# Weaving the attention of a chunk with the MLP of the chunk before it, in a four-layer transformer kernel on one core

## Chip, cores, metric

One core of one Trainium2 chip. The metric is device time in microseconds (us) of one execution, the median of several runs; profile times come from one profiled execution and are some 1.5 us shorter.

## The reference

Four layers on x of 2048 x 512, in bfloat16: attention A, MLP B, A, B, each with a LayerNorm ahead and a residual addition behind.

```python
def A(x):   # linear attention, 32 heads of 16
    q, k, v = split(x @ wqkv)
    phi(u) = concat(softmax(u @ w_phi), softmax(-u @ w_phi))       # per head, 32 features
    kv, z = phi(k)^T v, sum over s of phi(k)                       # needs ALL rows of x
    o = (phi(q) kv) / (phi(q) z + 1e-6)
    return o @ wo
def B(x):   # F = 1376
    return (relu(x @ W_gate) * (x @ W_up)) @ W_down
x = x + A(ln(x)); x = x + B(ln(x)); x = x + A(ln(x)); x = x + B(ln(x))
```

Two dependences matter. kv is a sum over all rows, so no query can be finished before all keys of the layer are. All else goes row by row, so the MLP of 512 rows (a chunk) can start when the attention of those rows is done.

## The kernel before

x lies in SBUF as 16 tiles of 128 rows, four to a chunk. The layers are traced one after the other. A list scheduler at build time turns the trace into one fixed order for each engine; what is traced earlier has precedence, and what is ready may overtake. At run time each engine works down its list.

```python
def ln_stats_chunk(st, c):            # one chunk: statistics of 4 tiles, then one inverse root for all 4
    ...
    rsqrt_dve(st, rstd[:], ve[:], TPC)            # 10 small VectorE operations
    ...
def layer_A(st):
    ...                                           # keys of 4 chunks; per chunk the sums are added to kvzacc in SBUF
    for c in range(NC):
        ...                                       # queries of chunk c+1 (prologue)
        for ti in range(TPC):
            kvq = st.ps_q.tile([P, 3, 512], F32, name="qps", tag="q")     # 3 PSUM banks, one buffer
            ...                                   # 9 matmuls, then on VectorE: rS, Tn, U, dd, o
            for b in range(NDB):
                nc.tensor.transpose(out=otps[:, b, :], in_=o[:, b * P:(b + 1) * P], identity=st.ident[:])
            nc.scalar.copy(out=oT[:], in_=otps[:])
            ...                                   # yps = oT.T @ wo, 4 matmuls
            nc.vector.tensor_tensor(out=st.X[:, t, :], in0=st.X[:, t, :], in1=yps[:], op=Alu.add)
def layer_B(st):
    for c in range(NC):
        ln_transpose_chunk(st, c, xnTB)           # LayerNorm, transposes by DMA
        for f in range(NFT):
            ...                                   # gps, ups (8 matmuls), rg = relu(gps), ru = ups, hT = rg * ru
        for ti in range(TPC):
            ...                                   # yps = hT.T @ wd (11 matmuls), X += yps
...
    run_layers(st, ("A", "B", "A", "B"))
```

The softmax here doesn't subtract the row's maximum and nothing guards it: scores larger than these inputs give would overflow.

## Time and profile before

| | us |
|---|---|
| median of three runs | 561.69 |
| range | 560.95 to 563.63 |
| profiled span | 560.4 |
| key sums of layer 1 ready | 98 |
| key sums of layer 2 ready | 350 |

The prediction below shows the activity map, the table by stage and the groups. In the map each digit is the busy share of an engine in a slice of 14 us, in tenths. PE is TensorE, DVE VectorE, ACT ScalarE, POOL GpSimd, SP the queue that issues DMAs; PEclk is the granted TensorE clock in tenths. What matters is that attention keeps VectorE busy and the MLP keeps TensorE busy.

### The profile page before, as it was taken

To read this page: it belongs to the slowest core of one execution; us is meant where nothing else is said; L and a number is where in the kernel's file an instruction comes from. 1 tells how busy PE (TensorE), PEld (TensorE's weight loads), DVE (VectorE), ACT (ScalarE), POOL (GpSimd) and SP (SyncE) were. 2 spreads that over 40 slices of the span, in tenths; PEclk is the share of its full clock that TensorE was granted. 3 is DMA by queue.
4 is the path that set the end of the run, shared out by engine and by line. 5 is a ranking of instruction groups with operands and counts; after the bars stand their busy time and mean duration, and the time that the engine had idled before them with its cause. 6 is when DMAs were issued, how large, how long until landed. Compare 5 with 4: busy or idle time off the path is not lost.

```text
span 560.4 us, 6418 instructions
## 1 busy us (share of the span) xinstructions
PE 439.0 (78%) x2304; PEld 211.2 (38%) x2304; DVE 349.6 (62%) x859; ACT 214.6 (38%) x401; POOL 67.7 (12%) x48
## 2 busy tenths in 40 slices
PE   0167789665756999999998799565766999999993
PEld 0033344332332444444443454333332444444441
DVE  4746986899887644463628976898888732222221
ACT  0044557131410625354444557131401625344440
POOL 4002674000000000000002774000000000000000
PEclk9999999689875999999999999687865999999998
DMA  8804200000001110230100200000001220200004
GB/s 292 311 0 85 47 20 2 0 0 1 1 11 28 37 39 1 48 66 1 37 2 6 34 1 0 1 0 2 0 10 29 38 39 0 39 0 2 0 1 150
DMA packets 40400, 19.34 MB, mean 35 GB/s; under 512 B 35008, under 2 KB 39120, under 8 KB 40368
## 3 DMA queue, kind: packets, MB, share of 16 engines
q1 hardware_dynamic: 38992, 12.59, 10.3%
q0 software_dynamic: 1376, 6.34, 3.1%
q8 instruction: 18, 0.29, 0.2%
q14 instruction: 14, 0.11, 0.1%
HBM read 8.44 MB, written 2.10 MB: 19 GB/s over the span
## 4 chain that ended last, share of the span: by engine, by line
PE 58%; DVE 18%; ACT 8%; DMA 8%; POOL 3%; issue 3%; SPq 1%; ACTq 0%; POOLq 0%; DVEq 0%
PE ups L187 14%; PE gps L183 13%; PE yps L199 9%; PE yaps L316 8%; DMA X<-in_A_x_dram 4%; POOL phiK L234 3%; ACT oT L313 3%; DVE sk L231 3%; PE pqps L268 3%; DMA xnTB<-xn 3%; PE otps L311 2%; PE kvq L243 2%; DVE o L307 2%; PE qps L283 2%; DVE X L318 2%
## 5 line engine op out<-in xcount | busy, mean ns | idle before, releaser
L193 DVE TENSOR_TENSOR hT<-rg,ru 128x512 bf16<-128x512 bf16 (+1 forms) x88 | 37.3, 424 | 95.3 <-ACT ru L192 95.3
L234 POOL TENSOR_TENSOR phiK<-ek,sk 128x1024 bf16<-128x1024 bf16 x32 | 61.3, 1928 | 276.1 <-ACT vext L222 256.0
L183 PE MATMUL gps<-xnTB,wg 128*128 128x512 bf16 (+1 forms) x352 | 92.1, 385 | 0.0
L187 PE MATMUL ups<-xnTB,wu 128*128 128x512 bf16 (+1 forms) x352 | 91.7, 383 | 0.4 <-DVE X L201 0.2
L190 ACT ACTIVATE rg<-gps 128x512 bf16<-128x512 f32 (+1 forms) x88 | 52.5, 597 | 85.8 <-PE gps L183 85.1
L199 PE MATMUL yps<-wd,hT 128*128 128x512 bf16 (+1 forms) x352 | 77.9, 379 | 1.8 <-DVE X L201 1.8
L316 PE MATMUL yaps<-wo,oT 128*128 128x512 bf16 x128 | 47.3, 509 | 24.2 <-ACT oT L313 24.2
L192 ACT CAST ru<-ups 128x512 bf16<-128x512 f32 (+1 forms) x88 | 51.5, 585 | 33.2 <-PE ups L187 33.2
L313 ACT COPY oT<-otps 128x512 bf16<-128x512 bf16 x32 | 19.1, 595 | 112.7 <-PE otps L311 112.7
L187 PEld LDWEIGHTS <-wu 128*128 128x128 bf16 (+1 forms) x352 | 35.2, 100 | 45.5 <-issue 4.4
L183 PEld LDWEIGHTS <-wg 128*128 128x128 bf16 (+1 forms) x352 | 35.8, 102 | 42.8 <-issue 3.2
L199 PEld LDWEIGHTS <-hT 128*128 128x128 bf16 (+1 forms) x352 | 34.4, 98 | 43.8 <-issue 2.6
L153 DVE BATCH_NORM_STATS2 bnst<-X 128x6 f32<-128x512 bf16 x64 | 43.3, 680 | 11.6 <-DMA X<-in_A_x_dram 11.2
L298 DVE TENSOR_TENSOR Tn<-qps,rS 128x1224 bf16<-128x1224 f32 x32 | 45.0, 1406 | 0.1
L168 DVE TENSOR_SCALAR xn<-X,mv,rstd 128x512 bf16<-128x512 bf16 x64 | 33.5, 535 | 17.4 <-DMA xnTB<-xn 11.8
L231 DVE TENSOR_REDUCE sk<-ek 128x64 f32<-128x1024 bf16 x32 | 38.2, 1195 | 6.5 <-ACT ek L229 6.2
L283 PE MATMUL qps<-R,EqT 128*128 128x144 bf16 x288 | 31.3, 270 | 13.6 <-DVE Tn L298 13.6
L220 PE MATMUL vps<-wqkv,xnTA 128*128 128x512 bf16 x128 | 36.2, 387 | 2.7 <-DMA xnTA<-xn 2.7
L201 DVE TENSOR_TENSOR X<-X,yps 128x512 bf16<-128x512 bf16 x32 | 21.8, 683 | 25.7 <-PE yps L199 25.7
L283 PEld LDWEIGHTS <-EqT 128*128 128x128 bf16 x288 | 26.4, 120 | 24.1 <-DVE Tn L298 16.5
L311 PE MATMUL otps<-ident,o 128*128 128x128 bf16 x128 | 15.2, 254 | 24.6 <-DVE o L307 24.6
L318 DVE TENSOR_TENSOR X<-X,yaps 128x512 bf16<-128x512 bf16 x32 | 22.0, 688 | 20.0 <-PE yaps L316 19.9
(60 smaller groups left out, 438.8 us busy)
## 6 DMA issues: line engine op xcount, KB each, us to landing
X<-in_A_x_dram SPq DMA_DIRECT2D x4, 512.0 KB, 9.6
out_dram<-X SPq DMA_DIRECT2D x1, 2048.0 KB, 7.5
wqkv<-in_A_wqkv_dram POOLq DMA_DIRECT2D x1, 1536.0 KB, 10.6
wg<-in_B_W_gate_dram POOLq DMA_DIRECT2D x1, 1376.0 KB, 14.3
wu<-in_B_W_up_dram POOLq DMA_DIRECT2D x1, 1376.0 KB, 17.7
wd<-in_B_W_down_dram POOLq DMA_DIRECT2D x1, 1280.0 KB, 20.8
wo<-in_A_wo_dram POOLq DMA_DIRECT2D x1, 512.0 KB, 11.5
xnTA<-xn SPq DMA_TRANSPOSE x32, 2.4
```

The costliest lines, as they stand in the source:

```text
L153: nc.vector.bn_stats(out=stats[:], in_=st.X[:, t, :])
L183: nc.tensor.matmul(gps[:fsz, :], lhsT=st.wg[:, b, f * P:f * P + fsz], rhs=xnTB[:, b, :], start=(b == 0), stop=(b == NDB - 1))
L187: nc.tensor.matmul(ups[:fsz, :], lhsT=st.wu[:, b, f * P:f * P + fsz], rhs=xnTB[:, b, :], start=(b == 0), stop=(b == NDB - 1))
L190: nc.scalar.activation(out=rg[:fsz, :], in_=gps[:fsz, :], func=AF.Relu)
L192: nc.scalar.copy(out=ru[:fsz, :], in_=ups[:fsz, :])
L193: nc.vector.tensor_tensor(out=hT[:fsz, f, :], in0=rg[:fsz, :], in1=ru[:fsz, :], op=Alu.mult)
L199: nc.tensor.matmul(yps[:], lhsT=hT[:fsz, f, ti * P:(ti + 1) * P], rhs=st.wd[:fsz, f, :], start=(f == 0), stop=(f == NFT - 1))
L231: nc.vector.tensor_reduce(out=sk[:], in_=ek[:].rearrange("p s (h f) -> p (s h) f", f=DH), axis=AX.X, op=Alu.add)
L234: nc.gpsimd.tensor_tensor(out=phiK[:, ti, :, :].rearrange("p s (h f) -> p (s h) f", f=DH), in0=ek[:].rearrange("p s (h f) -> p (s h) f", f ...
L283: nc.tensor.matmul(kvq[:, bank, slot * ERW:(slot + 1) * ERW], lhsT=EqT[:, b, s, ti * P:(ti + 1) * P], rhs=R[:, b, s, :, :].rearrange("p h ...
L298: nc.vector.tensor_tensor(out=Tn[:], in0=QV[:, :, :, 0:DH + 1], in1=rS[:].unsqueeze(3).to_broadcast([P, 3, 24, DH + 1]), op=Alu.mult)
L316: nc.tensor.matmul(yps[:], lhsT=oT[:, b, :], rhs=wo[:, b, :], start=(b == 0), stop=(b == NDB - 1))
```

## The change

The intent is to let the attention of a chunk run beside the MLP of the chunk before it, so that VectorE's work fills TensorE's stretch. Python generators yield after each group of matmuls with its cost, and `weave` traces two of them in proportion. Further: key sums stay in PSUM over all chunks, o is transposed by DMA in place of TensorE and ScalarE, LayerNorm goes tile by tile with the inverse root as a power on GpSimd, and the setup loads and folds weights in another order.

```diff
-def ln_transpose_chunk(st: KS, c: int, dst):
...
+def norm_tile(st, c, ti, dst):
...
+    nc.gpsimd.tensor_tensor(out=rstd[:], in0=ve[:], in1=st.nhalf[:, 0:1], op=Alu.pow)
+    xn = st.work.tile([P, D], BF16, name="xn")
+    nc.vector.tensor_scalar(out=xn[:], in0=x, scalar1=mv[:, 0:1], scalar2=rstd[:],
+                            op0=Alu.subtract, op1=Alu.mult)
+    nc.sync.dma_start_transpose(out=dst[:, :, ti * P:(ti + 1) * P], in_=xn[:])
...
+                mm = nc.tensor.matmul(self.kvq[:, g // 3, (g % 3) * GC:(g % 3 + 1) * GC], ...
+                                      start=(t == 0 and g % 3 == 0), stop=(t == st.T - 1),
...
-            for b in range(NDB):
-                nc.tensor.transpose(out=otps[:, b, :], in_=o[:, b * P:(b + 1) * P], identity=st.ident[:])
             oT = st.work.tile([P, NDB, P], BF16, name="oT")
-            nc.scalar.copy(out=oT[:], in_=otps[:])
+            nc.sync.dma_start_transpose(out=oT[:], in_=o[:])
+            yield 2.6
...
+def weave(main, main_cost, fill, fill_cost):
+    ...
+        if live_m and (not live_f or done_m / main_cost <= done_f / fill_cost):
+            ... done_m += next(main)
+        else:
+            ... done_f += next(fill)
+KC, QC, AC, BC = 41.2, 16.0, 26.4, 132.0
...
-    run_layers(st, ("A", "B", "A", "B"))
...
+    for (a, b, nxt) in ((A1, B1, A2), (A2, B2, None)):
+        run(a.queries(0))
+        run(a.queries(1))
+        a.build_R()
+        weave(a.attend(0), AC, seq(a.queries(2), a.queries(3)), 2 * QC)
+        weave(a.attend(1), AC, b.mlp(0), BC)
+        weave(a.attend(2), AC, b.mlp(1), BC)
+        weave(a.attend(3), AC, b.mlp(2), BC)
+        if nxt is not None:
+            weave(seq(nxt.keys(0), nxt.keys(1), nxt.keys(2)), 3 * KC, b.mlp(3), BC)
+            run(nxt.keys(3))
+        else:
+            run(b.mlp(3))
```

## The prediction

> **What bounds the kernel now.** I read the activity map first, since it shows stages, then a table of busy time by stage, then the costliest groups, and last the waits of the DMA queue and the timeline around the first matmuls of real work.
>
> From the page of the kernel before, 40 slices of 14 us each:
>
> ```profile
> PE   0167789665756999999998799565766999999993
> DVE  4746986899887644463628976898888732222221
> POOL 4002674000000000000002774000000000000000
> PEclk9999999689875999999999999687865999999998
> ```
>
> Two attention layers (slices 4 to 13 and 22 to 31) have VectorE at 8 to 9 tenths and TensorE at 5 to 7; two MLP layers (13 to 21, 31 to 39) have TensorE at 9 and VectorE at 2 to 6. The limit alternates. The stage table gives sizes: window, length, busy time of PE, PEld, DVE, ACT, POOL, then granted clock.
>
> ```profile
> 0.00:43.40 43.40, 12.23 (x64) 6.61 (x64) 22.64 (x117) 7.86 (x33) 6.45 (x16) 1.00 0.57 198
> 43.40:98.00 54.60, 45.76 (x289) 22.71 (x290) 44.17 (x68) 32.55 (x62) 30.67 (x16) 1.00 0.20 37
> 98.00:180.00 82.00, 50.60 (x306) 26.65 (x305) 70.15 (x157) 18.92 (x36) 0.00 (x0) 0.77 0.03 7
> 180.00:298.80 118.80, 117.67 (x530) 52.69 (x529) 61.03 (x183) 51.87 (x88) 0.00 (x0) 0.99 0.13 27
> 298.80:350.00 51.20, 43.92 (x290) 22.26 (x288) 41.49 (x72) 32.60 (x62) 30.63 (x16) 1.00 0.07 11
> 350.00:433.00 83.00, 51.95 (x306) 27.88 (x305) 70.27 (x156) 18.78 (x36) 0.00 (x0) 0.73 0.03 7
> 433.00:551.00 118.00, 116.91 (x529) 52.36 (x526) 39.18 (x108) 51.99 (x88) 0.00 (x0) 0.99 0.09 14
> ```
>
> Setup is 43 us; keys 54.6 and 51.2; attention 82 and 83, with VectorE 86% busy and a granted clock of 0.77 and 0.73; each MLP 118, TensorE 99% busy; output 9. TensorE does little in 165 us of attention, VectorE little in 237 us of MLP.
>
> The groups of instructions that set the price of a tile:
>
> ```profile
> L234 POOL TENSOR_TENSOR phiK<-ek,sk 128x1024 bf16<-128x1024 bf16 x32 | 61.3, 1928 | 276.1 <-ACT vext L222 256.0
> L316 PE MATMUL yaps<-wo,oT 128*128 128x512 bf16 x128 | 47.3, 509 | 24.2 <-ACT oT L313 24.2
> L298 DVE TENSOR_TENSOR Tn<-qps,rS 128x1224 bf16<-128x1224 f32 x32 | 45.0, 1406 | 0.1
> L231 DVE TENSOR_REDUCE sk<-ek 128x64 f32<-128x1024 bf16 x32 | 38.2, 1195 | 6.5 <-ACT ek L229 6.2
> ```
>
> The output projection costs 509 ns per matmul here against 383 in the MLP: the clock fell in the gaps.
>
> Setup, from the DMA queue's own waits and the timeline:
>
> ```profile
> SPq L170 <- DVE wT L97: 34.9, 1, 34.9
> ...
> 40.82 5.19 SPq L170 DMA_TRANSPOSE xnTA<-xn  x4
> ...
> 43.45 1.86 PE L220 MATMUL vps<-wqkv,xnTA 128*128 128x512 bf16 x4 [2.66 <-DMA xnTA<-xn]
> ```
>
> The first normalised tile was ready at 20.5 us, its transpose was issued at 40.8, just when the last matmul that read wT ended (37.42 + 3.36 in the timeline). The destination sits in a pool opened after the pool of wT was closed, so I infer that it reuses that memory and waits for it.
>
> **What the Trainium skill says.** "Perfetto Trace Analysis", section Optimization Strategy: where the most contended engine changes over time, interleaving the regimes may help. That is the change, and the stage table agrees that they differ. "TensorE: Matmul & The Clock Gate", section Back-to-back issue gap: N/2.4 + 2.5 ns, so 216 ns at N=512. The trace agrees: groups of four start 0.86 to 0.87 us apart in the MLP. The same page's clock-gate part says that idle TensorE falls to half rate; the attention stages' 0.77 and 0.73 agree. "SBUF — State Buffer", section Who interferes with whom: a VectorE operation in a 2-port mode, or with two SBUF inputs, and a GpSimd one that reads exclude each other for whole instructions; a reduce never contends. The trace agrees for xn: by stage,
>
> ```profile
> 43.40:98.00 54.60, 11.52 (x13) 1.00 0.20 37
> ...
> 180.00:298.80 118.80, 9.41 (x24) 0.99 0.13 27
> ```
>
> 0.89 us each beside GpSimd's multiplies, 0.39 without.
>
> **The change part by part.** Busy times of neighbours on VectorE overlap: o at 106.67 takes 0.69 and its successor starts at 107.28, so I take 0.08 off each mean for the time an operation really holds the engine.
>
> LayerNorm: the rsqrt chain of 11 small operations per chunk on VectorE (0.16 each, so 0.44 per tile) becomes one addition per tile (0.165) and a power on GpSimd. 0.28 saved x 64 tiles = 18 us of VectorE. Per tile: statistics 0.68, aggregate 0.17, addition 0.165, xn 0.39, less 4 x 0.08 = 1.1 us. No row or page prices the power; small GpSimd operations took 0.1 to 0.3, and I allow under 1.
>
> Key sums stay in PSUM: the 24 adds and copies per two layers (8.4 + 2.8 us) go, and the wait of the next chunk's key matmuls for them. Keys per tile on VectorE: LayerNorm 1.1, lock wait 0.5, reduce 1.14, reciprocal 0.47 = 3.2 us. On TensorE: 8 x 0.2165 + 8 x 0.065 = 2.25.
>
> Attention tile: 64 denominators in place of 72 and 1088 elements in place of 1224, but in two pieces: reciprocals 0.64, Tn 1.37, one U of 0.46 in place of 0.36 + 0.22, dd 0.33, o 0.66, X 0.69 = 4.15, less 8 x 0.08 = 3.5 us. TensorE: 8 small matmuls 0.58 + 0.87 = 1.45; the four transposes and ScalarE's copy (15.2 and 19.1 us in all) go. A DMA transpose (2.4 us landing, 1.2 issue) lengthens the latency by about 2 us against the transpose and copy, hidden where there is other work.
>
> MLP chunk: TensorE 29.1 (from 240.49 to 269.56 in the timeline). VectorE per tile: LayerNorm 1.1, hT 0.95, X 0.61 = 2.7, so 10.7.
>
> Now the stages. **Start to finished key sums of layer 1**: weights come in smaller loads, the key weights first, and the memory wait goes. Wk2 should be ready near 16 us (data about 5, sixteen transposes and matmuls and eight larger copies about 9). VectorE sets the rest: 16 x 3.2 = 51, preparation about 6, a first arrival at 4, some 5 idle, 2 for R: 68, against 98. That is 30 gained.
> **First chunk's attention**, with only two chunks of queries to fill: the old pace of 82/16 = 5.1 per tile, 20 us: 88.
> **Three woven phases**: TensorE 29.1 + 4 x 1.45 = 34.9, VectorE 14 + 10.7 = 25, so TensorE should bound. In-order engines and the layer norm chain at each boundary will cost; I take 37 each, and 4 for the first MLP's start: 115, so 203.
> **MLP of chunk 3 with keys of three chunks**: TensorE 12 x 2.25 + 29.1 = 56; VectorE 12 x 3.2 + 10.7 + about 5 of lock for hT = 54. Two engines both nearly full: 62, so 265.
> **Keys of chunk 3 and R**: the chain X, LayerNorm, transpose, keys, reduce, GpSimd, key sums, R after the last MLP tile: 16, so 281.
> **Layer 2 the same**: 20 + 115, so 416.
> **The last MLP**: 29.1 and a LayerNorm chain of 4, so 449; the output now leaves by tiles, about 4 in place of 9: 453. The measured time is 1.3 above the span: about 455.
>
> Check: TensorE's necessary work is 8 x 29.1 + 32 x 2.25 + 32 x 1.45 + 8 x 3.5 (queries) + 10 = 389; 455 has it 85% useful.
>
> **The rivals.** (1) VectorE's queue becomes the bound in the phases. It is in order ("TensorE: Matmul & The Clock Gate", section Architectural detail, calls ScalarE and VectorE strict FIFO), and the order is set at build time. If the X addition stands at its head waiting for a DMA transpose, the MLP's hT and so TensorE wait. Against: 25 of 35 us leaves slack. For: attention now shows 86% VectorE busy and still 5.1 us per tile, with one set of three PSUM banks. It would make phases of 42 rather than 37: 455 + 30 = 485. (2) GpSimd: a power that waits behind 1.93 us multiplies, or is slow itself, stalls xn and the transposes. For: it is in order too, and 0.89 us of xn shows what it does to VectorE. Against: GpSimd is 56 to 60% busy only in the key stages, empty in the six phases. Perhaps 10 us over the key stages: 465; if the power took several us, 480. (3) The weave works better than I allow: phases at TensorE's 34.9 and a start of 60 give 455 - 13 - 8 = 434. (4) The transposes by DMA form a new chain so long that the first-chunk stages grow from 20 to 25: 465.
>
> **Range and chances.** Rivals 1, 2 and 4 pull up, 3 down: 435 to 488 for 8 in 10. To be within 2% of 561.7 nearly all of the 107 us would have to fail; the setup alone gives 5%. Faster 0.97, same 0.02, slower 0.01.
>
> **What would show it.** Right: TensorE at 9 tenths from about 90 us to the end save one dip near 270 to 300; granted clock near 1 there; each phase 36 to 38 us; first key matmul near 16 us; R near 68; VectorE about 330 us busy; no wT wait of the transposes. Wrong: phases over 40 with TensorE waiting for ScalarE or VectorE while VectorE waits for yaps or oT (rival 1); xn waiting for a GpSimd power of over 1 us (rival 2); transposes landing well above 2.4 us (rival 4); a first key matmul after 30 us.

## More of the kernel before

Ratios are to the kernel before in the same rounds on the same chip. Differences in us between two edits often cross sets of runs, and each set ran on a chip of its own; the median of the kernel before differed by no more than 1 us between the sets.

## The result

The changed kernel takes 525.08 us in the median (523.89 to 526.72, four runs) against 562.66 of the kernel before. The ratio is 0.934 (95% interval 0.931 to 0.937). Ratios here are the mean time of one kernel's fast runs over that of the other's of the same rounds, so not quite the ratio of the medians. It is faster, and 70 us slower than the 455 predicted, outside the range.

The activity map of the changed kernel, slices of 13 us:

```profile
PE   0678877769949967996977988667994995997697
DVE  3978636765774677667856773776566467566122
POOL 3288640000000002004422552000000000000000
PEclk9989997789989997998999999778997999899699
```

TensorE stands at 9 in pairs of slices, with a 4 to 7 after it (slices 11, 14, 18 and again 30, 33, 36, counted from 0). VectorE is never at 9 after the keys of layer 1, so on average it has room in the phases. The table by stage (window, length, busy time of PE, PEld, DVE, ACT, POOL, clock) with windows cut at the first gate matmul of each MLP chunk:

```profile
0.00:76.70 76.70, 50.09 (x334) 28.19 (x341) 51.18 (x113) 34.63 (x65) 44.43 (x50) 0.96 0.48 138
76.70:112.20 35.50, 23.27 (x106) 10.41 (x107) 25.66 (x59) 12.90 (x25) 2.19 (x4) 0.80 0.15 30
112.20:156.30 44.10, 36.29 (x178) 17.27 (x182) 27.26 (x63) 13.00 (x22) 2.32 (x4) 0.93 0.12 25
156.30:200.90 44.60, 36.16 (x176) 17.21 (x180) 28.11 (x68) 12.99 (x22) 2.87 (x5) 0.92 0.12 24
200.90:245.30 44.40, 38.45 (x177) 17.33 (x180) 30.74 (x75) 16.15 (x28) 5.88 (x9) 0.96 0.18 36
...
489.10:523.70 34.60, 30.79 (x129) 13.55 (x132) 7.43 (x15) 12.99 (x22) 0.00 (x0) 0.93 0.05 16
```

A phase has 36 to 38 us of TensorE and 27 to 31 of VectorE and takes 44. Against the working of the prediction (all in us; the second layer's stages start at its first attention matmul, 322.5, and its first gate matmul, 358.0):

| stage | predicted | measured | difference |
|---|---|---|---|
| start to key sums of layer 1 | 68 | 76.7 | +8.7 |
| first chunk's attention, to the first gate matmul, layers 1 and 2 | 24 + 24 | 35.5 + 35.5 | +23 |
| three woven phases, layers 1 and 2 | 111 + 111 | 133.1 + 131.1 | +42.2 |
| MLP of chunk 3, keys and sums of layer 2 | 78 | 77.2 | -0.8 |
| last MLP and output (its LayerNorm chain counts with the phases above) | 37 | 34.6 | -2.4 |
| sum | 453 | 523.7 | +70.7 |

So nearly all of the miss is in the stages where attention meets the MLP. And the gain over the kernel before is mostly elsewhere: key sums of layer 1 are ready at 76.7 in place of 98 (21 us); from there to the key sums of layer 2, 245.8 in place of 252 (6 us); from there to the end, 201 in place of 210 (9 us, of which 6 are the output, 3.7 in place of 9.4 after the last matmul). The weaving, which was to give the most, shows about 10.

The timeline of the changed kernel at one boundary between phases (start, length, engine, what; in brackets the idle time ahead of it and what ended it). Of the names in it, gps and ups are the MLP's gate and up projections, ybps its down projection, and xnTB its normalised input; erq are attention's small matmuls of queries with key sums, Tn to o its steps on VectorE, oT the transposed o, and yaps its output projection:

```profile
183.25 7.30 PE L303 MATMUL ybps<-wd,hT 128*128 128x512 bf16 x33
...
189.89 1.21 SPq L261 DMA_TRANSPOSE oT<-o  x1
...
192.61 0.81 PE L265 MATMUL yaps<-wo,oT 128*128 128x512 bf16 x3 [1.61 <-DMA oT<-o]
...
193.46 0.69 DVE L268 TENSOR_TENSOR X_81<-X_81,yaps 128x512 bf16<-128x512 bf16 x1 [2.18 <-PE yaps L265]
...
194.98 0.98 DVE L250 TENSOR_TENSOR Tn<-erq,rS 128x816 bf16<-128x816 f32 x1
...
197.29 0.68 POOL L144 TENSOR_TENSOR rstd<-ve,nhalf 128x1 f32<-128x1 f32 x1 [9.16 <-DVE mv L140]
...
198.44 1.19 SPq L148 DMA_TRANSPOSE xnTB<-xn  x1
...
200.91 1.89 PE L286 MATMUL gps<-xnTB,wg 128*128 128x512 bf16 x4 [2.63 <-DMA xnTB<-xn]
```

From the phase's first gate matmul at 156.3 until the last down projection ends at 190.6, TensorE is nearly full: 34.3 us, where the prediction had 34.9. Then it stands, but for a few small matmuls, for 10.3 us. What it waits for can be read downward: the last tile's o goes through a DMA (189.9 to 192.4), the projection yaps, the addition to X, the LayerNorm (with Tn of the next chunk put between its steps on VectorE), the power, another DMA (198.4 to 200.9), and only then the first gate matmul. The four gate matmuls take 1.89 us in place of about 1.03 in mid-phase, at a granted clock of 0.50 (0.80 over the hole): the clock fell. "TensorE: Matmul & The Clock Gate" of the Trainium skill, section The HAM clock gate, says that an idle TensorE is clocked at half rate, and the 0.50 agrees.

My theory was then: the even weave ends attention and MLP together, so the last tile's chain has nothing left to cover it. Rivals: VectorE's list, the GpSimd power, or the DMA transpose of o as such.

### The profile page after: what moved, and what is told of

Read it like the earlier page. It is cut to its first block, busy times and chain, and to the rows that moved or that the text cites. A ratio compares the mean times of both kernels' runs of the same rounds, so it can differ in the third digit from the quotient of the medians.

```text
span 523.7 us, 6113 instructions
## 1 busy us (share of the span) xinstructions
PE 413.3 (79%) x2103; PEld 197.6 (38%) x2144; DVE 326.4 (62%) x719; ACT 194.3 (37%) x345; POOL 101.9 (19%) x114
## 4 chain that ended last, share of the span: by engine, by line
PE 52%; DVE 17%; DMA 12%; POOL 9%; issue 6%; ACT 3%; SPq 0%; POOLq 0%; ACTq 0%; DVEq 0%
PE gps L286 13%; PE ups L293 13%; PE ybps L303 9%; POOL phiK L188 7%; DMA oT<-o 6%; PE yaps L265 6%; PE qps L226 4%; DVE sk L184 3%; DVE Tn L250 3%; DMA xnTB<-xn 3%; PE erq L240 2%; DVE bnst L138 2%; DMA X_80<-in_A_x_dram 2%; POOL rstd L144 2%; PE kvq L196 2%
## 5 line engine op out<-in xcount | busy, mean ns | idle before, releaser
L144 POOL TENSOR_TENSOR rstd<-ve,nhalf 128x1 f32<-128x1 f32 x64 | 35.4, 561 | 334.8 <-DVE ve L142 313.5
L303 PE MATMUL ybps<-wd,hT 128*128 128x512 bf16 (+1 forms) x342 | 79.5, 379 | 0.5
L240 PE MATMUL erq<-R,Eq 128*128 128x144 bf16 x256 | 27.6, 248 | 29.5 <-DVE Tn L250 16.1
L250 DVE TENSOR_TENSOR Tn<-erq,rS 128x816 bf16<-128x816 f32 x64 | 45.8, 716 | 0.8
L226 PE MATMUL qps<-xnTA,Wq_334 128*128 128x512 bf16 x124 | 37.6, 435 | 2.3 <-ACT Eq L229 1.7
L240 PEld LDWEIGHTS <-Eq 128*128 128x128 bf16 x256 | 20.6, 108 | 41.8 <-DVE Tn L250 19.6
L174 ACT ACTIVATE ek<-kps 128x512 bf16<-128x512 f32 x32 | 19.3, 603 | 45.7 <-PE kps L171 42.3
L171 PE MATMUL kps<-Wk_123,xnTA 128*128 128x512 bf16 x124 | 35.4, 389 | 0.5 <-ACT ek L175 0.3
L179 PE MATMUL vps<-wv,xnTA 128*128 128x512 bf16 x124 | 34.1, 391 | 0.1
L249 DVE RECIPROCAL rS<-erq 128x48 f32<-128x48 f32 x64 | 22.4, 351 | 14.4 <-PE erq L240 14.4
```

Of the source, the lines that this page charges most:

```text
L144: nc.gpsimd.tensor_tensor(out=rstd[:], in0=ve[:], in1=st.nhalf[:, 0:1], op=Alu.pow)
L226: nc.tensor.matmul(qps[:], lhsT=st.Wq2[:, m, b * P:(b + 1) * P], rhs=self.xnT[c][:, m, :], start=(m == 0), stop=(m == NDB - 1))
L240: nc.tensor.matmul(kvq[:, bank, slot * ERW:(slot + 1) * ERW], lhsT=Eq[:, b, s, ti * P:(ti + 1) * P], rhs=st.R[:, g, :, :].rearrange("p h c ...
L250: nc.vector.tensor_tensor(out=Tn[:, :, lo:hi, :], in0=Q[:, :, :, 0:DH + 1], in1=rS[:, :, lo:hi].unsqueeze(3).to_broadcast([P, 2, hi - lo, ...
L303: nc.tensor.matmul(yps[:], lhsT=hT[:n, f, ti * P:(ti + 1) * P], rhs=st.wd[:n, f, :], start=(f == 0), stop=(f == NFT - 1))
```

## The experiments

All are edits of the changed kernel. "Before" lay between 562.67 and 563.61 us in each set. Every run passed the check of its result. That holds for freeln and freeln_petr too, which compute something else on purpose: the check does not tell them apart.

| run | edit | us | ratio to before |
|---|---|---|---|
| the change | | 525.08 | 0.934 |
| lead15 | attention leads the MLP by 1.5 | 490.89 | 0.871 |
| lead20 | by 2 | 488.54 | 0.868 |
| petr | o transposed by TensorE | 495.21 | 0.881 |
| petr_last, petr_rest | only tile 3, only tiles 0 to 2 of a chunk | 517.29, 512.01 | 0.920, 0.910 |
| noweave | no explicit weave | 495.83 | 0.881 |
| noweave_petr | both | 486.30 | 0.866 |
| freeln | MLP's LayerNorm input cut from attention (wrong) | 488.31 | 0.867 |
| freeln_petr | the same, o transposed by TensorE | 479.01 | 0.851 |
| lnin | LayerNorm traced inside attention | 540.35 | 0.960 |
| dversqrt, chunkrsqrt | power undone, per tile and per chunk | 570.71, 592.60 | 1.014, 1.053 |
| kvacc | key sums undone | 530.07 | 0.942 |
| lead15_petr_b | lead 1.5, o by TensorE | 474.13 | 0.842 |
| lnin_lead15_petr | and LayerNorm inside attention | 483.27 | 0.858 |
| lead15_petr_keyseq | lead 1.5, o by TensorE, keys not woven | 470.65 | 0.836 |
| lead20_petr_keyseq | the same, lead 2 | 469.76 | 0.836 |

### Attention traced ahead: lead15, lead20

```diff
-        weave(a.attend(1), AC, b.mlp(0), BC)
+        weave(a.attend(1), LEAD * AC, b.mlp(0), BC)      # LEAD = 1.5 or 2.0; the same for the other two
```

A larger cost for attention lets it be traced sooner: with 1.5 it is all traced when two thirds of the MLP are.

> Edit: in the six woven phases the attention of a chunk is traced 1.5 times as fast against the MLP, so that it is all traced when two thirds of the MLP are; nothing else differs. Theory (boundary chain): in each phase TensorE is full for 34.5 us and then stands for about 8 to 10 us, because the last attention tile, its X addition, LayerNorm and two DMA transposes follow the last down projection, with no matmuls left to cover them. With the lead about 12 us of MLP matmuls are left to cover that chain: phases of 36 to 38 us in place of 44, six or seven boundaries, so 475 to 492 us. Rivals: if the holes are VectorE's queue being full, or GpSimd's power, or PSUM banks, the lead moves work but not the holes: over 510 us.

> Edit: as the lead of 1.5, with a lead of 2. Dose and response: 1.0 gave 525 and 1.5 gave 491. Boundary theory: at 1.5 three of the four down projections, 7 us, already stand between the last output projection and the next gate matmul, which covers the chain of 6 to 8; more lead can cover little more: 484 to 494 us. Rival (attention should simply come first, the more the better): 475 us or less.

490.89 and 488.54 us, both inside what the boundary theory expected (475 to 492, 484 to 494). The timeline of lead15 at the same boundary:

```profile
175.31 1.20 SPq L261 DMA_TRANSPOSE oT<-o  x1
...
178.64 1.04 PE L265 MATMUL yaps<-wo,oT 128*128 128x512 bf16 x4 [1.20 <-DMA oT<-o]
...
179.51 7.30 PE L303 MATMUL ybps<-wd,hT 128*128 128x512 bf16 x33
...
187.15 1.03 PE L286 MATMUL gps<-xnTB,wg 128*128 128x512 bf16 x3
```

From yaps to gps it is 8.5 us, as before (8.3). But now three down projections lie behind yaps, and the gate matmul has no wait. The times from one chunk's first gate matmul to the next are 36 to 39 us in place of 43 to 45. The six phases together win 40 us; 9 of these are lost again from the start of MLP 3 to the first gate matmul of layer 2 (121.9 us in place of 112.6). Going from 1.5 to 2 gives no more than 2 us: the effect ends where the chain is covered. (lead15 once more, on another chip: 489.92 us, ratio 0.870.)

> MISLABELLED GUARD: this is the lead of 1.5 run again, to be timed beside the others on the same chip: 489 to 492 us as before.

### The wait itself taken away: freeln, freeln_petr

```diff
+    st.X.append(wo)                                   # a constant tile of X's shape
...
-            norm_tile(st, c, ti, xnT)
+            norm_tile(st, c if c == 0 else st.NC, ti, xnT)   # MLP only; the result is wrong on purpose
```

> Edit, with a wrong result on purpose: the MLPs of chunks 1, 2 and 3 normalise the constant tile wo (same shape, never written) in place of the chunk that attention has just updated. Same instructions and sizes; only the wait of the MLP's first matmul for the last attention tile is taken away, at six boundaries. Boundary theory: the phases fall from 44 to 36 us, six times 8: 472 to 487 us. Rival (the attention chain itself, with its DMA transposes, paces the phase): the phases stay over 41 us, 505 us or more.

> Edit: the same wrong-on-purpose cut, with o transposed by TensorE. Boundary theory: with the wait gone the latency of a DMA transpose has nothing to lengthen but the two unfilled first chunks: 4 to 10 us below the other cut. Rival (each transpose delays something of its own): 20 us or more below it.

488.31 us, one above the range of the boundary theory and far from the rival's 505. TensorE passes the boundary without a hole (timeline of freeln):

```profile
138.17 7.30 PE L304 MATMUL ybps<-wd,hT 128*128 128x512 bf16 x33
...
145.80 1.03 PE L287 MATMUL gps<-xnTB,wg 128*128 128x512 bf16 x4
```

In layer 1 the first gate matmuls of the four chunks come at 110.0, 145.8, 182.9 and 219.4: phases of 35.8, 37.1 and 36.5 us, which are the 37 of the prediction. In layer 2 they are 41.7, 37.3 and 35.6; why the first is longer was not followed up. With the same instructions, but without the LayerNorm's wait for attention, the predicted phase length appears in five of six, so this wait is what the phases lost. (Without the dependence the scheduler may also order the lists otherwise; lead15, which keeps it, gives nearly the same phases.) As in lead15, the way from MLP 3 to the next gate matmul gets longer, 119.3 us. With the wait gone, transposing o by TensorE gains 9 us (479.01), inside the 4 to 10 expected.

### Where the transpose of o matters: petr, petr_last, petr_rest

```diff
-            nc.sync.dma_start_transpose(out=oT[:], in_=o[:])
+            otps = st.ps_a.tile([P, NDB, P], BF16, name="otps", tag="a")
+            ...                                        # 4 transposes on TensorE
+            nc.scalar.copy(out=oT[:], in_=otps[:])     # petr_last: if ti == TPC - 1; petr_rest: if ti < TPC - 1
```

> Edit: o is transposed by TensorE and copied by ScalarE, as in the kernel before, in place of the DMA transpose; all else as in the changed kernel. Boundary-chain theory: the chain loses about 1.5 us per boundary and per tile of the unfilled first chunk (2.4 us landing plus issue against about 1.2 us), TensorE gains 128 small matmuls: 512 to 526 us. Rival (the DMA transpose of o is the cause of the missing gain): the holes go with it, under 500 us.

> Edit: only the last of the four tiles of each chunk has o transposed by TensorE and copied by ScalarE; the other three keep the DMA transpose. In the full undo the time went from 525 to 495 us. Theory (only the tile at the boundary matters, because its chain ends with nothing to cover it): most of the 30 us comes back, 495 to 508 us. Rival (each of the 32 transposes delays its neighbours, in the unfilled first chunk and by holding VectorE's or TensorE's queue): a quarter of it, 515 to 520 us.

> Edit: the mirror image: the first three tiles of each chunk are transposed by TensorE, the last by DMA. Boundary theory: little comes back, 512 to 522 us, what does coming from the two unfilled first chunks. Rival (every transpose counts alike): three quarters, 500 to 505 us.

petr gave 495.21: 30 us from a part that I had taken for 13 at most. Here the rival's expectation held, not mine. The timeline of petr at the boundary:

```profile
177.20 0.40 PE L263 MATMUL otps<-ident,o 128*128 128x128 bf16 x4
...
177.64 0.59 ACT L265 COPY oT<-otps 128x512 bf16<-128x512 bf16 x1 [8.18 <-PE otps L263]
...
178.30 1.03 PE L269 MATMUL yaps<-wo,oT 128*128 128x512 bf16 x4
...
179.16 1.68 PE L307 MATMUL ybps<-wd,hT 128*128 128x512 bf16 x7
...
187.30 0.58 PE L290 MATMUL gps<-xnTB,wg 128*128 128x512 bf16 x1
```

From the start of the transpose to yaps it is 1.1 us, against 2.7 from the DMA's issue to yaps in the changed kernel. A hole is left: the last down projection ends at 180.8, and but for a few small matmuls TensorE stands for 6.5 us, against 10.3. Three phases together take 119.7 us (109.1 to 228.8) in place of 133.1. That is 4.5 us a boundary in the mean (7.7 at the first, 2.8 and 2.9 at the others), more than the 1.6 of one transpose. In the changed kernel's list for TensorE, the small matmuls of tile 3 (erq) stand behind yaps of tile 2: in the timeline yaps at 181.66 waited 0.38 us for its DMA and erq followed at 182.75. So I read it that the chain to the boundary holds the transposes of the last two tiles, and that each undone transpose also lets the scheduler place other work; no run tests this. The split by tile says the same: tile 3 alone gave 8 us, tiles 0 to 2 gave 13, together 30. Both of my expectations for the split fell: it is not the last tile alone (495 to 508 expected, 517 measured), nor is it an equal share per tile (500 to 505 expected for three of four, 512 measured). Why the two together exceed their sum by 9 us I did not separate.

Whether the DMA transpose costs in itself or only at the boundary is told by the context: 30 us with the even weave, 9 with the wait cut, 16 with the lead (489.92 to 474.13 on one chip), 10 without a weave. Most of it belongs to the boundary.

> Edit: attention leads by 1.5, and o is transposed by TensorE. Each alone gave 34 and 30 us. Boundary theory: both shorten or cover the same holes, so together much less than the sum of 64: 475 to 488 us. Rival (two separate causes): 462 us or less.

474.13 us, one microsecond below the expected 475 to 488, and far above the 462 of two separate causes.

### No explicit weave: noweave, noweave_petr

```diff
-        weave(a.attend(1), AC, b.mlp(0), BC)
-        ...                                       # and the weave of keys with b.mlp(3)
+        for c in range(1, NC):
+            run(a.attend(c))
+        for c in range(NC):
+            run(b.mlp(c))
+        ...                                       # then the keys of the next layer
```

> Edit: all parts of the changed kernel, but traced one after the other: attention of all chunks, then the MLP of all chunks, then the keys of all chunks. Boundary-chain theory: the holes at the boundaries cost nearly as much as the weaving saves, so most of the measured gain comes from the setup (key sums ready at 77 us against 98) and the tail: 525 to 545 us, i.e. within 4 percent of the changed kernel. Rival (the weaving is what gave the 6.6 percent, the other parts nothing): 555 to 570 us.

> Edit: attention of all chunks traced ahead of all MLPs (no explicit weave) and o transposed by TensorE. Without the weave, DMA transposes gave 496; with the even weave and TensorE transposes 495; with the lead and TensorE transposes 474. Boundary theory: here the MLP never waits for the tile just finished, so as with the lead the undone transpose is worth only 8 to 16 us: 480 to 488 us. Rival (the transpose costs 30 us wherever it stands): about 466 us.

This was the largest surprise: 495.83 us, 29 faster than the woven kernel, where I expected 525 to 545. It does not mean that nothing is interleaved. The scheduler overlaps by readiness anyway, and attention traced first has precedence, so it runs ahead and the MLP fills its gaps: an unlimited lead. The first MLP chunk then takes 52 us with three chunks of attention inside it, the next two 31 and 32 us. noweave_petr at 486.30 fits the 480 to 488 of the boundary theory.

### The parts of LayerNorm and the key sums: dversqrt, chunkrsqrt, kvacc

```diff
-    nc.gpsimd.tensor_tensor(out=rstd[:], in0=ve[:], in1=st.nhalf[:, 0:1], op=Alu.pow)
+    rsqrt_dve(st, rstd[:], ve[:], 1)                  # dversqrt
...
-        for ti in range(TPC):
-            norm_tile(st, c, ti, xnT)
+        norm_chunk(st, c, xnT)                        # chunkrsqrt: the LayerNorm of the kernel before
...
+        for k in range(3):                            # kvacc: at the end of each chunk's keys
+            ... kvzacc = kvzacc + kvq
```

> Edit: the inverse root is computed on VectorE by the Newton steps of the kernel before, per tile, in place of the power on GpSimd. Boundary-chain theory: 10 small VectorE operations of about 0.15 us per tile replace a hop of about 0.9 us to GpSimd and back, so the chain gets about 0.5 us longer and VectorE's load grows by some 90 us times nothing where it is idle: 524 to 545 us. Rival (GpSimd's power behind the multiplies, or its hop, is the cause of the missing gain): 515 us or less.

> Edit: the LayerNorm of the kernel before, per chunk with Newton steps on VectorE for four tiles at once, in the changed kernel. The per-tile form of it cost 46 us. Per chunk it has a quarter of the operations (10 per chunk, about 26 us of VectorE in all), but a tile's transpose waits for all four tiles' statistics, which lengthens the chain at each boundary and at the start. Boundary theory: 530 to 550 us. If the 46 us were only the count of small operations: 520 to 532 us.

> Edit: the key sums are added to a SBUF tile after each chunk, as in the kernel before, with a single PSUM buffer, in place of staying in PSUM (one weight buffer of the setup is given up for the space). From the page of the kernel before: 24 adds and copies of 0.5 us and a wait of the next chunk's key matmuls for them. I expect 2 to 4 us per layer: 528 to 534 us; if it is on the path at each chunk, up to 540.

570.71 and 592.60: both undoings make the changed kernel slower than the kernel before (dversqrt by 1.4%, a difference that is clear of the noise but small), far above what I expected (524 to 545, 530 to 550). The rival that the power is the cause of the missing gain is dead; the power and the LayerNorm by tile are its condition. chunkrsqrt has fewer VectorE operations than dversqrt and is slower, so their count alone does not set the time. Its timeline shows the boundary:

```profile
225.91 1.05 DVE L167 TENSOR_SCALAR xn<-X,mv,rstd 128x512 bf16<-128x512 bf16 x3
...
227.35 5.15 SPq L169 DMA_TRANSPOSE xnTB<-xn  x4
...
233.92 1.86 PE L305 MATMUL gps<-xnTB,wg 128*128 128x512 bf16 x4 [1.38 <-DMA xnTB<-xn]
```

The four transposes follow each other after the last tile's statistics, in place of three being done long before. Phases take 41 to 55 us there. But the boundary is not all of it, and in dversqrt it is the smaller part. Split at key sums and first gate matmuls, dversqrt's 45 us (of the profiled span) lie 17 before the key sums of layer 1, 15 in the two first-chunk stages, 7 in MLP 3 with the keys, and 6 in the six phases; chunkrsqrt's 67 lie 14, 17, 9 and 28. So my boundary theory covers only a part of these two, and what the rest waits for was not followed up. The kernel before had the same LayerNorm, and its gate matmuls had no wait (0.0 us idle in its page); my explanation is that its attention was all done when the MLP began. kvacc costs 5 us (528 to 534 expected, 530.07 measured).

### LayerNorm traced inside attention: lnin, lnin_lead15_petr

```diff
             nc.vector.tensor_tensor(out=x, in0=x, in1=yps[:], op=Alu.add)
+            norm_tile(st, c, ti, self.mlp.xn[c])      # and no longer at the start of mlp(c)
             yield 4
```

> Edit: the MLP's LayerNorm of a tile is traced right behind that tile's X addition in attention, in place of at the start of the MLP, so that it comes before the next chunk's attention work in the order. From the last output projection to the first gate matmul the changed kernel takes 8.3 us, of which I count some 6 as bare durations and some 2 as next chunk's VectorE work put in between. Boundary theory: 1.5 to 3 us at each of six to eight boundaries, 502 to 516 us. Rival (the order on VectorE does not matter): 522 us or more.

> Edit: lead of 1.5, transposes by TensorE, and the LayerNorm traced in attention. The first two together gave 474. If the boundary holes are already covered, the third adds little: 466 to 475 us. If it finds holes still open, below 462 us.

Both missed: 540.35 where 502 to 516 was expected, and 483.27 where 466 to 475 was. At the boundary it did what I wanted: 7.0 us from yaps to the gate matmul in place of 8.3. But the phases stayed at 44 us, and 13 us were lost from the start of MLP 3 to the first gate matmul of layer 2 (125.6 in place of 112.6). What in that stretch loses them I did not follow up.

### The best version: lead15_petr_keyseq, lead20_petr_keyseq

```diff
-            weave(seq(nxt.keys(0), nxt.keys(1), nxt.keys(2)), 3 * KC, b.mlp(3), BC)
-            run(nxt.keys(3))
+            run(b.mlp(3))
+            for c in range(NC):
+                run(nxt.keys(c))
```

> Edit: as the version of 474 us, but the last MLP of layer 1 is traced before the keys of layer 2, not woven with them. If the key weave is useful (TensorE 56 and VectorE 54 us of work in the same stretch), undoing it costs 8 to 20 us: 482 to 494. If the order finds the overlap by itself, as it did without the other weaves: 470 to 478 us.

> Edit: the candidate version with the lead at 2 in place of 1.5: TensorE transposes, keys not woven. Boundary theory: 466 to 474 us, equal to the 470.7 of the lead of 1.5.

470.65 and 469.76 us. Undoing the key weave gained 3.5 us on top of lead and transpose (474.13, on another chip; ratios 0.842 and 0.836, whose intervals, 0.840 to 0.844 and 0.832 to 0.841, just overlap, so this gain is not certain). The groups of hT, first with the key weave, then without, give a likely part of it:

```profile
L301 DVE TENSOR_TENSOR hT<-rg,ru 128x512 bf16<-128x512 bf16 (+1 forms) x88 | 42.6, 484 | 43.5 <-ACT ru L300 42.3
```

```profile
L301 DVE TENSOR_TENSOR hT<-rg,ru 128x512 bf16<-128x512 bf16 (+1 forms) x88 | 36.1, 412 | 39.7 <-ACT ru L300 38.6
```

484 against 412 ns, 6 us of VectorE in all. hT has two SBUF inputs, and beside the keys GpSimd reads SBUF with its multiplies. "SBUF — State Buffer", section Who interferes with whom, says that these two exclude each other; the numbers agree. The profile by windows puts all of it there: the 11 hT of MLP 3 of layer 1 take 0.99 us each when woven with the keys and 0.40 when not; the other 77 take 0.41 in both kernels. The activity map of lead15_petr_keyseq, slices of 12 us:

```profile
PE   0559876779999999999996877686899999999996
PEclk9999899998999999999999999979999999999999
```

TensorE is at 9 through all woven stretches, and two stretches remain where it is not: the keys and the first chunk's attention of each layer.

## Why the prediction was wrong, point by point

- **What bounds each phase**: right within a phase. TensorE, with VectorE at 27 to 31 of 44 us (25 reckoned). Phases are over 40 as rival 1 had it, but TensorE waits at the boundary for a DMA of the LayerNorm chain, not for a full VectorE.
- **The term that failed: the boundary.** The step says "In-order engines and the layer norm chain at each boundary will cost; I take 37 each, and 4 for the first MLP's start". That is 2 us of hole on 34.9 of TensorE. Measured: 34.3 us full and a hole of 10.3, and phases of 43 to 45. freeln removed that wait and got phases of 36 to 37 in five of six. I had reckoned each engine's sum for the phase and not drawn the chain from the last o to the next gate matmul. Its parts could be had from the trace of before: two landings of 2.4, an addition, a LayerNorm, a projection, some 8 us by my estimate, at the one point where the even weave leaves no matmul over.
- **The DMA transpose**: the step says "hidden where there is other work". It is not hidden at the boundary; petr returned 30 us, and 9 with the boundary wait gone.
- **First chunk's attention**: 24 predicted, 35.5 measured in both layers. The second term that failed. Rival 4 had named the DMA transposes, but they land in 2.4 us (median), as before, and petr wins only 2 to 3 us here. In lead15_petr_keyseq the stage still takes 30.7 us in layer 1. TensorE's clock is 0.80 in that stage; of its waits in layer 1 the largest is 8.2 us for Tn, whose reads free the only buffer of erq. No edit tests this part; its cause stays open.
- **The setup**: direction and mechanism right (first key matmul at 18.9, predicted 16; before 45.1; the wait for the memory of wT is gone), size off by 9 us at the key sums. Some 3 of these are the late first key matmul; where the other 6 go was not followed up. VectorE's list puts statistics of chunk 1, waiting for its load, ahead of the copies that fold the key weights:

```profile
12.11 2.47 DVE L138 BATCH_NORM_STATS2 bnst<-X_80 128x6 f32<-128x512 bf16 x4 [1.77 <-DMA X_80<-in_A_x_dram]
...
16.40 1.01 PE L107 MATMUL tps<-ident,wk 128*128 128x128 bf16 x8 [9.72 <-DVE wT L108]
...
18.91 0.80 PE L171 MATMUL kps<-Wk_123,xnTA 128*128 128x512 bf16 x2
```

- **GpSimd's power**: "I allow under 1" was right, 0.56 us each, and rival 2 did not come. That it is worth 46 us in this order was not foreseen: I had priced it as 18 us of VectorE that is off the path.
- **VectorE in total**: 326 us busy, about 330 predicted. **MLP 3 with the keys**: 77.2 against 78, in part luck: where the boundary holes are covered or cut (lead15, freeln), this stage takes 85 to 86 us.
- **A reading of the map**: the prediction has TensorE at 5 to 7 tenths in the attention layers. That holds after the keys; in the key stage of layer 1 (slices 3 to 6 of its map, counted from 0) it is at 7 to 9. No term of the sum rests on it.
- **What decided the range**: the three woven terms carried an error of the same sign. A range that lets each of six boundaries cost 0 to 10 us would have reached 515 or so, and still not 525: the first-chunk stages added 23.

## What to carry to other kernels

When two stages are interleaved, sum the engines for the steady part, and then follow the one chain that crosses from one unit to the next, with every landing and hop at its measured length, and ask which work is left to cover it. Let the stage that feeds the next unit run ahead by at least that chain (here a lead of 1.5 took 34 us off), rather than end both together. A transfer of 2.4 us that is free in mid-stream is on the path at the seam, and a scheduler left to fill gaps by precedence may do better than an even weave by hand.

## What the Trainium skill lacked or had wrong

- "Perfetto Trace Analysis", section Optimization Strategy: it says that interleaving regimes may help, and nothing of how they must be offset. Here an even interleave took 525 us, the same with attention leading by 1.5 took 491, and none by hand 496.
- "GPSIMD Engine Reference": no cost of a power. One of 128x1 took 0.56 us (64 of them, 35.4 us).
- "DMA: Bandwidth & Descriptors", section DMA Transpose (X-bar): no latency of a small transpose there (the page's section Anatomy of one DMA has a fixed cost of about 2 us, fitted on DMAs that GpSimd issues). One of 128x512 in SBUF held the queue 1.2 us and landed about 2.4 us after its issue; by TensorE and ScalarE, transpose start to next matmul was 1.1 us.
